# Talking-heads attention and a squared-ReLU FFN on one core: reciprocals by pairs, new lengths for SyncE in the planner, evictions on either engine, AV in one piece

## The chip, the cores and the metric

The kernel runs on one core of one Trainium2 chip. The metric is the device time in microseconds; a kernel's time is the median over several executions. One further execution is recorded by the hardware profiler, and every duration below is from that recording.

## The reference

Inputs are `q`, `k`, `v` (8 batches, 12 heads, 448 rows, 64 wide), two 12x12 head-mixing matrices and the two weight matrices of the FFN (768x2048, 2048x768).

```
scores = 0.125 * q @ k^T                       # per batch and head, 448 x 448
scores = einsum('bhij,hg->bgij', scores, w_pre)
attn   = exp(scores - max(scores)); attn /= sum(attn) + 1e-9
attn   = einsum('bhij,hg->bgij', attn, w_post)
x      = (attn @ v), heads side by side        # 3584 x 768
out    = (max(x @ w_in, 0) ** 2) @ w_out
```

## The kernel before

The 448 rows of a batch are cut into 45 **chunks** of ten rows (one of them has eight), and a chunk holds its rows for all twelve heads, 120 partitions by 448 keys. 8 batches make 360 chunks, numbered n. Each goes through a fixed chain (`chunk`, L734):

- TensorE mixes the heads (`f_m`, L774, into a bank of PSUM). Its input is an `sch` tile that SyncE's DMA has gathered from `snat`, the scores by heads (`relayout`, L686; the DMA is issued in `move`, L679). The scores come from `score` (L640) and are copied out of PSUM to `snat` on VectorE or ScalarE (L666). `snat` has two buffers, `sch` eleven. The 26 steps "direct" in batch 0 skip the relayout (L780).
- VectorE takes the row minimum of the negated scores (`f_max`, L785), ScalarE the exponential with its row sum (`f_exp`, L788; an instruction that reads the accumulator follows each), VectorE the reciprocal (`f_rc`, L794), GpSimd scales the second mixing matrix with it (`f_wq`, L797).
- TensorE multiplies by that, "AT", four matmuls (`f_at`, L804), and VectorE or ScalarE copies the result to `atb` (`f_ac`).

The tiles between the steps (`es`, `mn`, `sm`, `rc`, `wq`) have NE = 6 buffers each, so the mix of chunk n needs the AT of chunk n-6.

When the chunks of half a batch are through, `av` (L832) multiplies by `v` in three pieces of 16 matmuls (batch 0: smaller ones, more often). A piece fills one bank, and ScalarE copies it to `xt` (L853). The FFN runs over units of 128 or 256 columns of `xt` (`unit`, L879): first matmul (L896), ReLU on ScalarE (L909), square on GpSimd (L912), second matmul (L928), a copy to `osb` on VectorE (L943), store by SyncE. FFN matmuls have the lowest priority: they fill TensorE where no chunk is ready.

The order on each engine is written by a **planner** (`Planner.run`, L135), at build time. It replays all operations with a cost in ns, a latency, a priority and dependencies. At each point an engine takes the ready operation of least priority value. An operation with two costs, such as `{"DVE": 540, "ACT": 440}`, goes to whichever of the two engines takes it first. The chip then runs each engine's list in that order, whatever the real durations are: an instruction that waits holds up all that stand behind it on its engine. The planner's guess for the chunk's relayout on SyncE is 770 or 500 ns (L712). AHEAD (L43) says how many chunks ahead relayouts and scores are ranked.

TensorE's score matmuls of 64 rows work in row mode and AV's of 64 columns in column mode. The planner charges TURN = 95 ns for a change, and STAY lets TensorE, once in row mode, take further scores ahead of other work (L211 to L222). Where TensorE has nothing ready early in the run, the planner may put in idle matmuls (`still`, L1145). In banks, `MOST` caps the kinds, and an operation that needs several banks waits until all are free at once.

Of the kernel before, what the change touches and what calls it, by code (L numbers as in the profile page):

```python
# [24 lines left out]
CI = 10  # L25
# [9 lines left out]
NB = 4  # L35
# [6 lines left out]
NSCH = 11  # L42
AHEAD = 7.2  # L43
FIFO = 50
# [3 lines left out]
TURN = 95  # L48
STAY = 2
HOLD = "g"  # L50
# [65 lines left out]
class Planner:  # L116
# [18 lines left out]
    def run(self):  # L135
# [39 lines left out]
        while True:  # L175
            for eng, heap in ready.items():
# [24 lines left out]
                while heap:  # L201
                    item = heapq.heappop(heap)
                    op = item[2]
                    if op.eng is not None:
                        continue
                    wide = len(op.bank) > 1
                    if not fits(op) or (short and op.bank and op.bank[0][0] in HOLD):
                        short = short or wide
                        kept.append(item)
                        continue  # L210
                    if eng == "PE" and mode == ROWS and op.mode != ROWS and first is None:  # L211
                        first = item
                        kept.append(item)
                        continue
                    if first is not None:
                        if op.mode != ROWS or op.pri > first[0] + STAY:
                            kept.append(item)
                            if op.pri > first[0] + STAY:
                                op, item = first[2], first
                                kept.remove(first)  # L220
                            else:
                                continue  # L222
                    args = []
                    break
                else:
                    item = None
                    if first is not None:
                        kept.remove(first)
                        item, op, args = first, first[2], []
# [68 lines left out]
def kernel(  # L298
# [33 lines left out]
    mn = many(NE, "mn", [KC, 1], F32)  # L332
    sm = many(NE, "sm", [KC, 1], F32)
    rc = many(NE, "rc", [KC, 1], F32)
    wq = many(NE, "wq", [KC, H, CI], BF16)
# [227 lines left out]
    def x_tail(b):  # L563
        old = [score_ops[b - 1, 0, p] for p in range(NPAIR)]

        def turn():
            nc.sync.dma_start(
                out=zt[:, :, :], in_=qt[:, :, :].rearrange("p a c -> p (a c)"), transpose=True,
            )

        pri = b * NCHUNK - 15
        op = add("SP", 1250, pri, turn, [tail_in[b]] + old)
        done = add("TURN", 800, pri, lambda: None, [op], lat=6000)
        got_tail[b] = [done]
        for p in range(NPAIR):
            ready_tail[b, p] = done
# [8 lines left out]
    def x_piece(b, g):  # L585
# [30 lines left out]
        ]  # L616
        sk = add("SP", TURN_SP, pri, turn_k, ck + old)
        sq = add("SP", TURN_SP, pri, turn_q, cq + old)
        k_ = tk_op[2 * b + g] = add("TURN", 1500, pri, lambda: None, [sk], lat=6000)
# [66 lines left out]
    def relayout(b, c):  # L686
# [8 lines left out]
        if r == 2 and cc == 0:  # L695
            src_of[n] = schl
            here.append(move(n, pri, 700, deps + side.get(b - 1, []), schl[24:96, :], sn[120:126, :, :], lat))
            return
# [12 lines left out]
        for of, r0, r1, srcs in parts:  # L711
            ns = 770 if r1 - r0 > 90 else 500  # L712
            relay_of.setdefault(of, []).append(move(n, pri, ns, deps + old, src_of[n][r0:r1, :], srcs, lat))
# [20 lines left out]
    def chunk(b, c):  # L734
# [52 lines left out]
        def f_exp():  # L787
            nc.scalar.activation(  # L788
                out=es[i][0:rows, 0:S], in_=slots[mk][0:rows, 0:S], func=ACT.Exp, scale=-1.0,
                bias=mn[i][0:rows, 0:1], accum_out=sm[i][0:rows, 0:1],  # L790
            )

        def f_rc():
            nc.vector.reciprocal(out=rc[i][0:rows, :], in_=sm[i][0:rows, :])  # L794

        def f_wq():
            nc.gpsimd.tensor_scalar(  # L797
                out=wq[i][0:rows, :, 0:ns], in0=back[0:rows, :, 0:ns], scalar1=rc[i][0:rows, 0:1], scalar2=1.0,
                op0=ALU.mult, op1=ALU.mult,
            )  # L800
# [24 lines left out]
        e = exp_op[n] = add("ACT", 626, n + 0.4, f_exp, [x, at_op.get(n - NE), rc_op.get(n - NE)], lat=190, frees=mk)  # L825
        s_ = rc_op[n] = add("DVE", 75, n + 0.2, f_rc, [e, wq_op.get(n - NE)], lat=180)
        w = wq_op[n] = add("POOL", 370, n + 0.5, f_wq, [s_, at_op.get(n - NE)] + (backed if not far else []), lat=70)
# [3 lines left out]

    def av(b, half, g, x0, x1):  # L832
        to = [(max(c0, x0), t0 + max(x0 - c0, 0), min(c0 + w, x1) - max(c0, x0)) for c0, t0, w in spans(b % 2, half)]
        to = [span for span in to if span[2] > 0]
        key = ("g", "v", b, half, g, x0)

        def mms(slot):
            v_ = slot[:, :].rearrange("p (a c) -> p a c", a=2)
            for i in range(2):
                c2 = 2 * g + i  # L840
                for jb in range(NB):
                    for hh in range(2):
                        nc.tensor.matmul(  # L843
                            v_[64 * hh:64 * hh + 64, i, 0:x1 - x0],
                            lhsT=vs[:, 2 * c2 + hh, jb, :],
                            rhs=atb[half][:, jb, 2 * c2 + hh, x0:x1],
                            start=(jb == 0), stop=(jb == NB - 1),
                        )

        def evac():  # L850
            v_ = slots[key][:, :].rearrange("p (a c) -> p a c", a=2)
            for c0, t0, w in to:
                nc.scalar.copy(out=xt[:, 2 * g:2 * g + 2, t0:t0 + w], in_=v_[:, :, c0 - x0:c0 - x0 + w])  # L853

# [5 lines left out]
        if b >= 2:  # L860
# [4 lines left out]
        mm = add(  # L865
            "PE", 60 + 48 * (x1 - x0) // 14, pri, keep(key, mms), [ac_op[n] for n in cs] + v_in[b] + old, lat=200,
            bank=key, mode=COLS,
        )
        av_op.setdefault((b, half), []).append(mm)
        xc = add("ACT", 440 if len(to) == 1 else 650, pri, evac, [mm], lat=100, frees=key)  # L870
        for _, t0, w in to:
            xc_op.setdefault(b // 2, []).append((t0, t0 + w, xc))

# [5 lines left out]
    def unit(pair, ui):  # L879
# [11 lines left out]
        for f0 in range(0, FT, nf):  # L891
# [15 lines left out]

            def relu(key=key, gi=gi):
                nc.scalar.activation(out=hr[gi % 2][:, :], in_=slots[key][:, :], func=ACT.Relu)  # L909

# [6 lines left out]

            rl = add("ACT", 500, 0, relu, [end, hr_log[gi - 2] if gi >= 2 else None], lat=100, frees=key)
            sq = add("POOL", 1020, FILL, square, [rl] + old_o, lat=70)
            hr_log.append(sq)  # L920
            sq_op[ix].append(sq)
        for mt in range(w // 128):
            for nt in range(2):
# [17 lines left out]

                def evac(key=key, si=si, nt=nt):
                    nc.vector.tensor_copy(out=osb[si % 2][:, nt * 384:(nt + 1) * 384], in_=slots[key][:, 0:384])  # L943

                ev = add("DVE", 480, 0, evac, [end, st_op.get(si - 2)] + ([m_op[n_] for n_ in direct] if si < 2 else []), lat=100, frees=key)
                whole = not (z == W2B and mt == 1 and pair == B // 2 - 1)
                evs = evs + [ev] if nt == 1 and whole else [ev]
                if nt == 1 or not whole:
                    done = []
                    for rows, dst, o in pieces(pair, a + mt * 128, None if whole else nt):  # L950
                        def store(dst=dst, o=o, rows=rows, si=si, e0=0 if whole else nt * 384, e1=384 if not whole and nt == 0 else DMODEL):
                            nc.sync.dma_start(out=dst, in_=osb[si % 2][o:o + rows, e0:e1])
                        done.append(add("SP", 450 if rows <= CI else 850, FILL, store, evs))
                    st_op[si] = pl.moved("DMA", 8, 140, 130, 0, done, 1500)
# [105 lines left out]
    def first_batch():  # L1060
# [7 lines left out]
        for n, c in enumerate(ORDER0):  # L1068
# [16 lines left out]
            if c == C0[1]:  # L1085
                for g in range(3):
                    av(0, 0, g, 0, P_ROWS)
                unit(0, 0)
            if c == C0[2]:
                for g in range(3):  # L1090
                    av(0, 0, g, P_ROWS, XA)
            if c == C0[3]:
                for g in range(3):
                    av(0, 1, g, 0, P_ROWS)
                unit(0, 1)
        for g in range(3):
            av(0, 1, g, P_ROWS, XB)
        unit(0, 2)

    def next_batch(b):  # L1100
# [11 lines left out]
        for r in range(NJ + 1):  # L1112
            for p in groups(b, r):
                score(b, r, p)
            for c in range(C0[r], (C0 + [NCHUNK])[r + 1]):
                relayout(b, c)
                chunk(b, c)
                if c == C0[2]:
                    for g in range(3):
                        av(b, 0, g, 0, XA)  # L1120
                    unit(b // 2, 0 if b % 2 == 0 else last - 1)
                if b + 1 < B and c in (3, 6):
                    load_ahead(b + 1, n0 + c, 0 if c == 3 else 6)
        for g in range(3):
            av(b, 1, g, 0, XB)
        unit(b // 2, 1 if b % 2 == 0 else last)
# [59 lines left out]
```

## Time and profile before

| what | value |
|---|---|
| median of 3 runs | 587.76 us (587.71 to 588.72) |
| the profiled execution's own time | 588.38 us |
| its span, first to last instruction | 586.6 us |
| TensorE busy | 571.7 us (97%), 5809 matmuls |
| VectorE, ScalarE, GpSimd busy | 488.5, 469.6, 323.5 us |
| granted TensorE clock | 1.000 |

In a group of instructions the columns are line, engine, operation, output<-input, shape and count, then busy us and the mean ns of one. In the timeline the first two numbers are start and length in us, and what stands in brackets is the idle time before and what ended it. "PEld" is TensorE's weight load, "SPq" an instruction of SyncE that issues a DMA.

### The profile page before, as it was taken

How to read it: one execution, taken by the hardware profiler on the slowest of the kernel's cores; microseconds unless marked ns; L12 is line 12 of the kernel's file. 1: busy time of each engine (PE TensorE's matmuls, PEld its weight loads, DVE VectorE, ACT ScalarE, POOL GpSimd, SP SyncE). 2: the span in 40 equal slices, each digit the busy share in tenths (PEclk: the TensorE clock that was granted, in tenths of full speed). 3: DMA queues.
4: the chain of work that ended last, by engine and by line, in shares of the span. 5: the costliest groups of instructions: out<-in, count | busy, mean ns of one | idle time of the engine just before them, and what ended most of it. 6: DMA issues, size and time to landing. Idle time of an engine off the chain costs nothing.

```text
span 586.6 us, 17120 instructions
## 1 busy us (share of the span) xinstructions
PE 571.7 (97%) x5809; PEld 410.3 (70%) x5809; DVE 488.5 (83%) x1256; ACT 469.6 (80%) x1238; POOL 323.5 (55%) x592
## 2 busy tenths in 40 slices
PE   8999999999999999999999999999999999999996
PEld 5658666776677667667768676767757776767783
DVE  4899989987799897999898998999899897989201
ACT  2689998988888888787899889878888988888330
POOL 7366356655576347736586356834577444735340
PEclk9999999999999999999999999999999999999999
DMA  9989949964599549974398548964399545322021
GB/s 119 213 149 225 174 99 201 182 146 112 117 193 138 147 142 156 167 164 121 97 189 176 151 122 130 194 146 121 85 185 185 140 131 121 114 77 85 2 55 54
DMA packets 132996, 81.01 MB, mean 138 GB/s; under 512 B 60484, under 2 KB 127916, under 8 KB 132908
## 3 DMA queue, kind: packets, MB, share of 16 engines
q1 hardware_dynamic: 85340, 57.11, 40.1%
q0 software_dynamic: 47568, 22.81, 30.5%
q8 instruction: 45, 0.74, 0.5%
q14 instruction: 43, 0.35, 0.2%
HBM read 45.70 MB, written 11.01 MB: 97 GB/s over the span
## 4 chain that ended last, share of the span: by engine, by line
PE 78%; DMA 8%; DVE 6%; ACT 4%; issue 2%; POOL 2%; SPq 0%; DVEq 0%; ACTq 0%; POOLq 0%
PE bank L928 24%; PE bank L896 20%; PE bank L804 11%; PE bank L774 10%; PE bank L843 6%; PE bank L652 5%; DMA ks<-in_k_dram 4%; DMA sch<-snat 3%; ACT es L788 2%; DVE mn L785 2%; PE bank L780 1%; DVE snat L452 1%; DVE atb L452 1%; ACT hr L909 1%; PE bank L508 1%
## 5 line engine op out<-in xcount | busy, mean ns | idle before, releaser
L788 ACT ACTIVATE es<-bank,mn 120x448 bf16<-120x448 f32 (+1 forms) x360 | 229.9, 645 | 30.9 <-DVE mn L785 23.4
L797 POOL TENSOR_SCALAR wq<-wback,rc 120x120 bf16<-120x120 f32 (+1 forms) x347 | 125.8, 366 | 174.2 <-DVE rc L794 102.0
L785 DVE TENSOR_REDUCE mn<-bank 120x1 f32<-120x448 f32 (+1 forms) x360 | 210.6, 611 | 5.1 <-PE bank L774 2.4
L928 PE MATMUL bank<-w,h 128*128 128x384 bf16 x896 | 173.5, 325 | 0.3
L896 PE MATMUL bank<-xt,w 128*128 128x256 bf16 (+1 forms) x1632 | 165.0, 254 | 0.2
L452 DVE CAST atb<-bank 112x480 bf16<-112x480 f32 (+3 forms) x226 | 137.5, 619 | 27.6 <-PE bank L804 25.9
L896 PEld LDWEIGHTS <-w 128*128 128x128 bf16 x1632 | 135.6, 98 | 22.1 <-issue 3.6
L912 POOL TENSOR_TENSOR h<-hr 128x512 bf16<-128x512 f32 x112 | 116.2, 1039 | 48.9 <-ACT hr L909 46.2
L804 PEld LDWEIGHTS <-es 120*112 120x112 bf16 (+1 forms) x1440 | 114.8, 129 | 40.2 <-issue 10.2
L804 PE MATMUL bank<-wq,es 120*112 120x120 bf16 (+1 forms) x1440 | 127.5, 217 | 5.4 <-POOL wq L797 3.8
L928 PEld LDWEIGHTS <-h 128*128 128x128 bf16 x896 | 84.2, 97 | 54.6 <-issue 4.2
L774 PE MATMUL bank<-sch,wmix 120*128 120x448 bf16 x339 | 107.7, 353 | 0.8 <-DVE snat L452 0.6
L452 DVE CAST snat<-bank 128x448 bf16<-128x448 f32 x159 | 93.2, 613 | 6.1 <-DMA sch<-snat 3.1
L454 ACT CAST atb<-bank 112x480 bf16<-112x480 f32 (+3 forms) x158 | 84.0, 543 | 14.4 <-PE bank L804 13.5
L909 ACT ACTIVATE hr<-bank 128x512 f32<-128x512 f32 x112 | 67.3, 601 | 32.2 <-PE bank L896 25.9
L454 ACT CAST snat<-bank 128x448 bf16<-128x448 f32 x165 | 82.0, 550 | 8.6 <-PE bank L652 5.1
L788 ACT ACTIVATION_READ_ACCUMULATOR es<-bank,mn 120x1 f32 (+1 forms) x360 | 76.2, 212 | 0.0
L794 DVE RECIPROCAL rc<-sm 120x1 f32<-120x1 f32 (+1 forms) x360 | 53.5, 154 | 13.6 <-ACT es L788 10.8
L943 DVE COPY osb<-bank 128x384 f32<-128x384 f32 x56 | 30.9, 552 | 31.9 <-PE bank L928 31.5
L774 PEld LDWEIGHTS <-wmix 120*128 120x128 bf16 (+1 forms) x347 | 31.4, 97 | 20.1 <-issue 12.5
L843 PE MATMUL bank<-atb,vs 112*64 112x192 bf16 (+3 forms) x864 | 40.6, 250 | 0.1
L843 PEld LDWEIGHTS <-vs 112*64 112x64 bf16 x864 | 36.6, 110 | 4.0 <-issue 3.5
(60 smaller groups left out, 280.7 us busy)
## 6 DMA issues: line engine op xcount, KB each, us to landing
sch<-snat SPq DMA_DIRECT2D x324, 105.0 KB
out_dram<-osb SPq DMA_DIRECT2D x22, 360.0 KB
vs<-in_v_dram POOLq DMA_DIRECT2D x16, 336.0 KB, 7.7
ks<-in_k_dram POOLq DMA_DIRECT2D x14, 336.0 KB, 9.8
qs<-in_q_dram POOLq DMA_DIRECT2D x14, 288.0 KB, 9.1
w<-in_moe_w_in_dram POOLq DMA_DIRECT2D x6, 512.0 KB, 14.2
w<-in_moe_w_out_dram POOLq DMA_DIRECT2D x4, 768.0 KB, 21.6
out_dram<-osb SPq DMA_DIRECT2D x10, 192.0 KB
```

The costliest lines, as they stand in the source:

```text
L452: nc.vector.tensor_copy(out=out_, in_=in_)
L454: nc.scalar.copy(out=out_, in_=in_)
L774: nc.tensor.matmul(slot[:, 0:S], lhsT=wm[0:rows, :], rhs=src[0:rows, :], start=True, stop=True,)
L785: nc.vector.tensor_reduce(out=mn[i][0:rows, :], in_=slots[mk][0:rows, 0:S], axis=AX.X, op=ALU.min)
L788: nc.scalar.activation(out=es[i][0:rows, 0:S], in_=slots[mk][0:rows, 0:S], func=ACT.Exp, scale=-1.0, bias=mn[i][0:rows, 0:1], accum_out=sm ...
L797: nc.gpsimd.tensor_scalar(out=wq[i][0:rows, :, 0:ns], in0=back[0:rows, :, 0:ns], scalar1=rc[i][0:rows, 0:1], scalar2=1.0, op0=ALU.mult, op ...
L804: nc.tensor.matmul(slot[0:P_KEYS, jb * H * ns:(jb + 1) * H * ns], lhsT=es[i][0:rows, jb * P_KEYS:(jb + 1) * P_KEYS], rhs=wq[i][0:rows, :, ...
L843: nc.tensor.matmul(v_[64 * hh:64 * hh + 64, i, 0:x1 - x0], lhsT=vs[:, 2 * c2 + hh, jb, :], rhs=atb[half][:, jb, 2 * c2 + hh, x0:x1], start ...
L896: nc.tensor.matmul(slot[:, j * w:(j + 1) * w], lhsT=w1[c2][:, (f0 + j) * 128:(f0 + j + 1) * 128], rhs=xt[:, c2, a:z], start=(c2 == 0), sto ...
L909: nc.scalar.activation(out=hr[gi % 2][:, :], in_=slots[key][:, :], func=ACT.Relu)
L912: nc.gpsimd.tensor_tensor(out=h2_[:, f0:f0 + nf, 0:w], in0=hr[gi % 2][:, :].rearrange("p (f c) -> p f c", f=nf), in1=hr[gi % 2][:, :].rear ...
L928: nc.tensor.matmul(slot[:, 0:384], lhsT=h2_[:, ft, mt * 128:(mt + 1) * 128], rhs=w2[:, ft, nt * 384:(nt + 1) * 384], start=(ft == 0), stop ...
```

## The change

Five edits. (1) Chunks n and n+1 (n even) share `sm` and `rc` tiles with two columns; one reciprocal of 120x2 runs after both exponentials. (2) Planner costs of SyncE's instructions: relayout 770 to 860 and 500 to 590, the extra one 700 to 780, transposes 1250 to 1400 and 1500 to 1600..2300, stores 450 to 510 and 850 to 930; AHEAD 7.2 to 7.6. (3) ReLU, `xt` copies and `osb` copies may run on either engine. (4) From batch 3 (the fourth) on, AV is one operation that takes three banks. (5) STAY holds for column mode too, with 6.

```diff
-AHEAD = 7.2
+AHEAD = 7.6
-STAY = 2
+GS, ONE = [(0, 1, 2)], [(0,), (1,), (2,)]
+STAY = {ROWS: 2, COLS: 6}
...
-                    if eng == "PE" and mode == ROWS and op.mode != ROWS and first is None:
+                    if eng == "PE" and mode and op.mode != mode and first is None:
...
-                        if op.mode != ROWS or op.pri > first[0] + STAY:
+                        if op.mode != mode or op.pri > first[0] + STAY[mode]:
...
-        op = add("SP", 1250, pri, turn, [tail_in[b]] + old)
+        op = add("SP", 1400, pri, turn, [tail_in[b]] + old)
...
-        sk = add("SP", TURN_SP, pri, turn_k, ck + old)
-        sq = add("SP", TURN_SP, pri, turn_q, cq + old)
+        sk = add("SP", 2300 if b == 2 else TURN_SP + 300, pri, turn_k, ck + old)
+        sq = add("SP", 2000 if b == 2 else TURN_SP + 100, pri, turn_q, cq + old)
...
-            ns = 770 if r1 - r0 > 90 else 500
+            ns = 860 if r1 - r0 > 90 else 590
...
-            nc.vector.reciprocal(out=rc[i][0:rows, :], in_=sm[i][0:rows, :])
+            nc.vector.reciprocal(out=rc[i // 2][:, :], in_=sm[i // 2][:, :])
...
-        s_ = rc_op[n] = add("DVE", 75, n + 0.2, f_rc, [e, wq_op.get(n - NE)], lat=180)
+        if n % 2 == 0:
+            s_ = rc_op[n] = add("DVE", 77, n + 0.2, f_rc, [e, wq_op.get(n - NE), wq_op.get(n - NE + 1)], lat=180)
+        else:
+            s_ = rc_op[n] = rc_op[n - 1]
+            s_.left += 1
+            e.next.append(s_)
...
-        xc = add("ACT", 440 if len(to) == 1 else 650, pri, evac, [mm], lat=100, frees=key)
+        for g, key in zip(gs, keys):
+            xc = add(
+                {"ACT": 440, "DVE": 540} if len(to) == 1 else {"ACT": 650, "DVE": 750}, 0, pri,
+                lambda eng, g=g, key=key: evac(eng, g, key), [mm], lat=100, frees=key,
+            )
...
+            def relu(eng, key=key, gi=gi):
+                if eng == "DVE":
+                    nc.vector.tensor_scalar(
+                        out=hr[gi % 2][:, :], in0=slots[key][:, :], scalar1=0.0, scalar2=0.0, op0=ALU.max, op1=ALU.add,
+                    )
+                else:
+                    nc.scalar.activation(out=hr[gi % 2][:, :], in_=slots[key][:, :], func=ACT.Relu)
...
-            rl = add("ACT", 500, 0, relu, [end, hr_log[gi - 2] if gi >= 2 else None], lat=100, frees=key)
+            rl = add({"ACT": 500, "DVE": 590}, 0, 0, relu, [end, hr_log[gi - 2] if gi >= 2 else None], lat=100, frees=key)
...
-                ev = add("DVE", 480, 0, evac, [end, st_op.get(si - 2)] + ([m_op[n_] for n_ in direct] if si < 2 else []), lat=100, frees=key)
+                ev = add({"DVE": 480, "ACT": 440}, 0, 0, evac, [end, st_op.get(si - 2)] + ([m_op[n_] for n_ in direct] if si < 2 else []), lat=100, frees=key)
...
-                        done.append(add("SP", 450 if rows <= CI else 850, FILL, store, evs))
+                        done.append(add("SP", 510 if rows <= CI else 930, FILL, store, evs))
...
-                    for g in range(3):
-                        av(b, 0, g, 0, XA)
+                    for gs in GS if b >= 3 else ONE:
+                        av(b, 0, gs, 0, XA)
```

More of the change, by code (lines that the diff above doesn't have):

```diff
@@ L215, in run @@
                     if first is not None:
-                        if op.mode != ROWS or op.pri > first[0] + STAY:
+                        if op.mode != mode or op.pri > first[0] + STAY[mode]:
                             kept.append(item)
-                            if op.pri > first[0] + STAY:
+                            if op.pri > first[0] + STAY[mode]:
                                 op, item = first[2], first
@@ L332 @@
     mn = many(NE, "mn", [KC, 1], F32)
-    sm = many(NE, "sm", [KC, 1], F32)
-    rc = many(NE, "rc", [KC, 1], F32)
+    sm = many(NE // 2, "sm", [KC, 2], F32)
+    rc = many(NE // 2, "rc", [KC, 2], F32)
     wq = many(NE, "wq", [KC, H, CI], BF16)
@@ L696, in relayout @@
             src_of[n] = schl
-            here.append(move(n, pri, 700, deps + side.get(b - 1, []), schl[24:96, :], sn[120:126, :, :], lat))
+            here.append(move(n, pri, 780, deps + side.get(b - 1, []), schl[24:96, :], sn[120:126, :, :], lat))
             return
@@ L789, in f_exp @@
                 out=es[i][0:rows, 0:S], in_=slots[mk][0:rows, 0:S], func=ACT.Exp, scale=-1.0,
-                bias=mn[i][0:rows, 0:1], accum_out=sm[i][0:rows, 0:1],
+                bias=mn[i][0:rows, 0:1], accum_out=sm[i // 2][0:rows, i % 2:i % 2 + 1],
             )
         def f_rc():
-            nc.vector.reciprocal(out=rc[i][0:rows, :], in_=sm[i][0:rows, :])
+            nc.vector.reciprocal(out=rc[i // 2][:, :], in_=sm[i // 2][:, :])
         def f_wq():
             nc.gpsimd.tensor_scalar(
-                out=wq[i][0:rows, :, 0:ns], in0=back[0:rows, :, 0:ns], scalar1=rc[i][0:rows, 0:1], scalar2=1.0,
+                out=wq[i][0:rows, :, 0:ns], in0=back[0:rows, :, 0:ns], scalar1=rc[i // 2][0:rows, i % 2:i % 2 + 1], scalar2=1.0,
                 op0=ALU.mult, op1=ALU.mult,
@@ L830, in chunk, with av, mms, evac @@
         ac_op[n] = add({"DVE": 565 * len(where), "ACT": 600 * len(where)} if len(where) == 1 else {"DVE": 700, "ACT": 850}, 0, n + 1.6, f_ac, [a], lat=110, frees=ak)
-    def av(b, half, g, x0, x1):
+    def av(b, half, gs, x0, x1):
         to = [(max(c0, x0), t0 + max(x0 - c0, 0), min(c0 + w, x1) - max(c0, x0)) for c0, t0, w in spans(b % 2, half)]
         to = [span for span in to if span[2] > 0]
[L835 to L850, printed above, removed]
+        keys = [("g", "v", b, half, g, x0) for g in gs]
+        def mms(*got):
+            for g, slot in zip(gs, got):
+                v_ = slot[:, :].rearrange("p (a c) -> p a c", a=2)
+                for i in range(2):
+                    c2 = 2 * g + i
+                    for jb in range(NB):
+                        for hh in range(2):
+                            nc.tensor.matmul(
+                                v_[64 * hh:64 * hh + 64, i, 0:x1 - x0],
+                                lhsT=vs[:, 2 * c2 + hh, jb, :],
+                                rhs=atb[half][:, jb, 2 * c2 + hh, x0:x1],
+                                start=(jb == 0), stop=(jb == NB - 1),
+                            )
+        def evac(eng, g, key):
             v_ = slots[key][:, :].rearrange("p (a c) -> p a c", a=2)
             for c0, t0, w in to:
-                nc.scalar.copy(out=xt[:, 2 * g:2 * g + 2, t0:t0 + w], in_=v_[:, :, c0 - x0:c0 - x0 + w])
+                copy(eng, xt[:, 2 * g:2 * g + 2, t0:t0 + w], v_[:, :, c0 - x0:c0 - x0 + w])
         def touches(c):
@@ L865, in av @@
         mm = add(
-            "PE", 60 + 48 * (x1 - x0) // 14, pri, keep(key, mms), [ac_op[n] for n in cs] + v_in[b] + old, lat=200,
-            bank=key, mode=COLS,
+            "PE", 60 + 48 * (x1 - x0) // 14 * len(gs), pri, keep(keys, mms), [ac_op[n] for n in cs] + v_in[b] + old, lat=200,
+            bank=keys, mode=COLS,
         )
         av_op.setdefault((b, half), []).append(mm)
-        xc = add("ACT", 440 if len(to) == 1 else 650, pri, evac, [mm], lat=100, frees=key)
-        for _, t0, w in to:
-            xc_op.setdefault(b // 2, []).append((t0, t0 + w, xc))
+        for g, key in zip(gs, keys):
[3 more added lines that the diff above has]
+            )
+            for _, t0, w in to:
+                xc_op.setdefault(b // 2, []).append((t0, t0 + w, xc))
     def units_of(pair):
@@ L906, in unit @@
             gi = len(hr_log)
-            def relu(key=key, gi=gi):
-                nc.scalar.activation(out=hr[gi % 2][:, :], in_=slots[key][:, :], func=ACT.Relu)
+            def relu(eng, key=key, gi=gi):
+                if eng == "DVE":
+                    nc.vector.tensor_scalar(
+                        out=hr[gi % 2][:, :], in0=slots[key][:, :], scalar1=0.0, scalar2=0.0, op0=ALU.max, op1=ALU.add,
+                    )
+                else:
+                    nc.scalar.activation(out=hr[gi % 2][:, :], in_=slots[key][:, :], func=ACT.Relu)
             def square(gi=gi, f0=f0):
@@ L940, in unit, with evac @@
                 si = ix_store[0]
-                def evac(key=key, si=si, nt=nt):
-                    nc.vector.tensor_copy(out=osb[si % 2][:, nt * 384:(nt + 1) * 384], in_=slots[key][:, 0:384])
-                ev = add("DVE", 480, 0, evac, [end, st_op.get(si - 2)] + ([m_op[n_] for n_ in direct] if si < 2 else []), lat=100, frees=key)
+                def evac(eng, key=key, si=si, nt=nt):
+                    copy(eng, osb[si % 2][:, nt * 384:(nt + 1) * 384], slots[key][:, 0:384])
+                ev = add({"DVE": 480, "ACT": 440}, 0, 0, evac, [end, st_op.get(si - 2)] + ([m_op[n_] for n_ in direct] if si < 2 else []), lat=100, frees=key)
                 whole = not (z == W2B and mt == 1 and pair == B // 2 - 1)
@@ L1085, in first_batch @@
             if c == C0[1]:
-                for g in range(3):
-                    av(0, 0, g, 0, P_ROWS)
+                for gs in ONE:
+                    av(0, 0, gs, 0, P_ROWS)
                 unit(0, 0)
             if c == C0[2]:
-                for g in range(3):
-                    av(0, 0, g, P_ROWS, XA)
+                for gs in ONE:
+                    av(0, 0, gs, P_ROWS, XA)
             if c == C0[3]:
-                for g in range(3):
-                    av(0, 1, g, 0, P_ROWS)
+                for gs in ONE:
+                    av(0, 1, gs, 0, P_ROWS)
                 unit(0, 1)
-        for g in range(3):
-            av(0, 1, g, P_ROWS, XB)
+        for gs in ONE:
+            av(0, 1, gs, P_ROWS, XB)
         unit(0, 2)
@@ L1118, in next_batch @@
                 if c == C0[2]:
-                    for g in range(3):
-                        av(b, 0, g, 0, XA)
+                    for gs in GS if b >= 3 else ONE:
+                        av(b, 0, gs, 0, XA)
                     unit(b // 2, 0 if b % 2 == 0 else last - 1)
@@ L1123, in next_batch @@
                     load_ahead(b + 1, n0 + c, 0 if c == 3 else 6)
-        for g in range(3):
-            av(b, 1, g, 0, XB)
+        for gs in GS if b >= 3 else ONE:
+            av(b, 1, gs, 0, XB)
         unit(b // 2, 1 if b % 2 == 0 else last)
```

## The prediction

> **What bounds the kernel now.** I read the busy shares first, then busy time by stage, then the timeline of the worst stage. The page:
>
> ```profile
> PE 571.7 (97%) x5809; PEld 410.3 (70%) x5809; DVE 488.5 (83%) x1256; ACT 469.6 (80%) x1238; POOL 323.5 (55%) x592
> ```
>
> TensorE is the bound, so only its own work and its waits count. Its work: in the chain of waits 12 matmuls of the first FFN product at 256 columns take 1.31 us (109 ns each), 64 of the second take 10.41 (163 ns). With the spacings that the timeline shows for the others (52 ns a matmul of AT, 189 a mix, 95 a row-mode score, some 40 us for AV) all 5809 come to about 529 us. The 182 changes of tile mode cost 0.145 us each (starts of matmuls across a change, less the spacing), 26 us. 1.1 us lie before the first matmul and 5.0 behind the start of the last. That is 561 of 586.6; of the other 25, 10 fall into the first 20 us (loads, and matmuls spaced 0.37 instead of 0.19 us). The rest are waits and small gaps. Busy time in stretches (length; then PE, PEld, DVE, ACT, POOL):
>
> ```profile
> 20.00:47.00 27.00, 25.41 (x232) 16.82 (x231) 26.06 (x77) 22.44 (x61) 12.80 (x26) 1.00 1.03 182
> 47.00:82.00 35.00, 33.35 (x530) 25.26 (x530) 32.24 (x85) 33.57 (x94) 19.08 (x36) 1.00 0.97 182
> 82.00:130.00 48.00, 47.93 (x522) 33.41 (x520) 42.81 (x112) 43.20 (x116) 27.64 (x54) 1.00 0.89 162
> 130.00:145.00 15.00, 13.84 (x125) 9.63 (x122) 11.82 (x31) 11.97 (x32) 9.01 (x14) 1.00 0.46 127
> 145.00:215.00 70.00, 69.50 (x706) 49.24 (x706) 61.71 (x159) 61.14 (x163) 38.57 (x73) 1.00 0.79 144
> 215.00:245.00 30.00, 28.16 (x278) 20.60 (x277) 25.54 (x67) 24.59 (x64) 22.00 (x38) 1.00 0.97 159
> 245.00:350.00 105.00, 105.00 (x1054) 76.06 (x1054) 97.81 (x248) 89.91 (x242) 57.15 (x108) 1.00 0.71 146
> ```
>
> TensorE is idle for 1.6, 1.7, 0.1, 1.2, 0.5, 1.8 and 0.0 us, and after 350 us for 0.5. A matmul's record hides up to 0.2 us of each wait; by starts, gaps of over 0.14 us beyond spacing and mode change sum to 2.3, 3.3, 0.4, 1.7, 1.3, 2.9, 0.1 and 1.6: **13.7 us**. That is all that any reordering can win in the middle, and past 245 us almost nothing is left. In 20 to 47 us VectorE is busy 97%: the chain of waits runs through it there. The stretch from 130 us is of another kind:
>
> ```profile
> 135.68 4.29 SPq L680 DMA_DIRECT2D sch<-snat  x5
> ...
> 138.21 0.97 ACT L454 CAST snat<-bank 128x448 bf16<-128x448 f32 x2 [1.90 <-DMA sch<-snat]
> 138.23 1.16 DVE L452 CAST snat<-bank 128x448 bf16<-128x448 f32 x2 [2.21 <-DMA sch<-snat]
> 138.80 0.49 PEld L804 LDWEIGHTS <-es 120*112 120x112 bf16 x8 [1.13 <-ACT snat L454]
> ```
>
> SyncE issues five relayouts in 4.29 us, 858 ns each; the planner counted 770. So `snat` is freed later than planned, both copying engines stand 2 us at an instruction that wants its buffer, and TensorE behind them 1.1.
>
> **The change, part by part.** The sum goes against the profiled execution's 588.38 us; the median shown is 0.62 lower.
>
> *TensorE's own list.* The built order holds the same matmuls plus four idle ones (35 to 39; they fill waits, 0). Mode changes fall from 182 to 178: 4 x 0.145 = **-0.6 us** (bounds 0 and -0.8). That is all of the column STAY and of AV in one piece, since in 17 of 19 visits to column mode the 48 matmuls of three pieces already stood together; what was to be gathered is gathered. The Trainium skill, "TensorEngine Tiling (Array Packing)", Key Properties, says that a change of tiling mode drains TensorE; the 0.145 us agree, and by that rule too the saving is four drains. Holding three banks at once is cost 0: FFN work covers it, and without that cover it is at most the 0.4 us of one eviction for each of ten gathered AVs, whose users stand behind other FFN work in the order.
>
> *SyncE's lengths.* Nothing is removed; the planner now spaces relayouts as the chip does (858 against 860). What should go are gaps that follow a late relayout: those at 130 to 145 us (1.7), at 145 to 215 (1.3; the chain there leads through relayouts of 7.56 and 1.56 us), and 1.4 of the 3.3 in 47 to 82, behind one of 7.32. Together 4.4 us. But the transfers stay, and SyncE's queue was issuing 18 of 20 us at 200 to 220 us, so the next burst is late by whatever else lands late. I take half: **-2.2 us** (bounds -4.4 and +1, one such gap newly made).
>
> *Reciprocals by pairs.* A reciprocal's record is 154 ns, but VectorE starts the next instruction 70 ns on (135.33 and 135.40 in the timeline). 180 fewer free 12.6 us of VectorE, 0.9 of it in the stretch where it is the chain (13 pairs x 70 ns). Against that, every even chunk waits for the odd one's sum: the two reciprocals were 1.34 us apart in the mean, and half of the ATs stood under 0.9 us behind their `wq`. In the new order the AT moves back too: between mix and AT of an even chunk stand 6.8 us of TensorE's work in the median (5.4 before), of an odd one 6.0 (5.5). The ring of six covers it: chunks are 1.51 us apart, six are 9.05. Only in batch 0, where few fillers exist, may it cost; the five shortest stretches there, against a chain of 2.4 us (0.61 + 0.65 + 0.2 + 0.15 + 0.37 and hand-overs), lack 0.9 us more than before. The 0.9 freed and the 0.9 lacked cancel: **0** (bounds -0.9 and +1.5).
>
> *ReLU, `xt`, `osb` on either engine.* The order puts 86 of 112 ReLUs on VectorE, 29 of 63 `xt` copies too, 22 of 56 `osb` copies on ScalarE; 29 fewer `atb` and 7 fewer `snat` copies on VectorE. Starts back to back: a copy of 384 takes VectorE 463 ns, of 448 522, so a ReLU of 512 is estimated at 581 (ScalarE: 478). VectorE: 86 x 0.581 + 12.5 for `xt` - 12.6 for reciprocals - 29 x 0.56 - 7 x 0.522 - 22 x 0.463 = **+20 us**; ScalarE -27. In the trace VectorE thus goes from 467 to 487 us of slots, no bound over the span. But to the 45th row minimum it is 68.1 before and 71.4 after, to the 90th 123.4 and 128.5. FFN work covers that from batch 1 on, not where VectorE is 92% to 97% busy. There are no ReLUs before 47 us; from 47 to 82 us ScalarE, which gives them up, is the fuller of the two (33.57 of 35 against 32.24). I go by that row: **0** (bounds -1.5, if the freer ScalarE shortens waits, and +3.3, all of batch 0's rise). The Trainium skill, "VectorE: DVE Perf Modes", Why PSUM operands drop a tier, holds fp32 from PSUM at one element a cycle; it speaks against moving ReLU there, and the slower VectorE row (463 for 384) agrees. It changes nothing in the 581.
>
> Sum: -0.6 - 2.2 + 0 + 0 = **-2.8 us**: 585.6 for a profiled execution, **585.0** against the median.
>
> **Rivals.**
>
> *VectorE becomes the chain in batches 0 and 1 (slower).* To the 90th row minimum it has 138 us (11 to 149 us); its slots go from 89% to 93% of that. ReLUs in its queue wait for the end of FFN matmuls (ScalarE spent 9.6 us so between 20 and 550 us, at 0.5 each), and row minima stand behind them. Price: half of the 5.1 us of added slots, 2.5, and the even chunks' 0.9; the gain at SyncE is lost to it, -0.6 stays: +2.8, or 590.5; with half of SyncE's gain 589.4. It decides if over half of the added slots land where TensorE has no FFN work. For: 97% and 92% busy; against: the planner sees these lengths, and ScalarE takes other copies.
>
> *Nothing moves (the relabelled lengths shift gaps but do not close them).* Those at 215 to 245 us (2.9) follow a load of `k` that lands 9.8 us after issue, which no edit touches; if SyncE's gaps reappear elsewhere, -0.6 remains: 587.2.
>
> *All goes well.* SyncE's whole 4.4, 0.9 at the reciprocals, 1.5 from ScalarE, 0.6: -7.4, 580.4. For: later stages show gaps near 0 with the same work; against: half of the gaps are in batch 0, where VectorE gets more.
>
> **How the numbers follow.** Forecast (583 to 586.5) 0.50; all well (under 583) 0.14; nothing (586.5 to 588.9) 0.17; VectorE (over 588.9) 0.19. The range to hold 8 in 10: 581.8 to 589.2, which leaves out the ends of "all well" and of VectorE's case. A difference of under 0.2% (1.2 us) could not be told from no change here: faster (under 586.6) 0.64, same 0.17, slower 0.19.
>
> **What would show it.** Right: TensorE's 26 us of mode changes nearly unchanged; in a stretch at 130 to 145 us no copy to `snat` idle for 2 us behind a relayout; VectorE's busy time up by some 10 us in spite of 120 fewer instructions, ScalarE's down by 30; the ReLU's mean on VectorE near 670 ns; a `k` load still stalling around 225 to 240 us. Wrong: row minima queued behind waiting ReLUs, and batch 1's first row minimum, now at 82.0 us, at 84 or later (VectorE's case); ATs that wait for `wq` more than the page's few us (pairs); new idle of `snat` copies behind DMA (SyncE).

## The result, and the profile after

The changed kernel takes 585.15 us in the median of 17 runs (584.19 to 587.03), the kernel before 587.76 (586.21 to 590.83); the ratio is 0.9950, 95% interval 0.9937 to 0.9963. The forecast was 585.0 us, and faster. The profiled execution took 585.32 us, its span is 583.5 (586.6 before).

The busy shares of the changed kernel:

```profile
PE 569.2 (98%) x5813; PEld 407.5 (70%) x5813; DVE 510.9 (88%) x1136; ACT 443.2 (76%) x1179; POOL 321.7 (55%) x591
```

VectorE's busy time rose by 22.4 us with 120 instructions fewer, ScalarE's fell by 26.4. Busy time by stretches, in the columns used before:

```profile
20.00:47.00 27.00, 25.38 (x234) 16.27 (x233) 25.79 (x70) 22.65 (x62) 12.82 (x25) 1.00 1.05 188
47.00:82.00 35.00, 32.80 (x527) 25.04 (x525) 33.34 (x78) 30.60 (x84) 18.49 (x35) 1.00 0.95 176
82.00:130.00 48.00, 46.87 (x521) 32.94 (x519) 45.53 (x104) 41.24 (x112) 28.19 (x57) 1.00 0.95 167
130.00:145.00 15.00, 15.00 (x142) 10.95 (x140) 14.60 (x32) 12.31 (x32) 9.92 (x15) 1.00 0.40 109
145.00:215.00 70.00, 69.63 (x705) 48.95 (x704) 65.45 (x146) 57.07 (x154) 38.20 (x73) 1.00 0.71 151
215.00:245.00 30.00, 29.21 (x291) 21.45 (x290) 28.84 (x63) 24.84 (x66) 23.02 (x39) 1.00 0.96 161
```

TensorE's idle time went from 1.2 us to nothing at 130 to 145 us and from 1.8 to 0.8 at 215 to 245; it rose from 1.7 to 2.2 at 47 to 82 and from 0.1 to 1.1 at 82 to 130. At 138 us, where copies to `snat` had stood for 2 us, the timeline now reads:

```profile
136.66 5.17 SPq L681 DMA_DIRECT2D sch<-snat  x6
...
138.07 1.14 DVE L453 CAST snat<-bank 128x448 bf16<-128x448 f32 x2
...
138.29 0.96 ACT L455 CAST snat<-bank 128x448 bf16<-128x448 f32 x2
```

No bracket stands behind either copy: neither waits for a relayout. Six relayouts took 5.17 us, 862 ns each, just what the planner now counts.

Most of the rise at 82 to 130 us is at one place. The timeline there:

```profile
81.58 0.69 DVE L921 TENSOR_SCALAR hr<-bank 128x512 f32<-128x512 f32 x1 [0.74 <-PE bank L907]
...
82.19 0.65 DVE L453 CAST atb<-bank 112x480 bf16<-112x480 f32 x1
...
82.67 0.23 ACT L789 ACTIVATION_READ_ACCUMULATOR es<-bank,mn 120x1 f32 x1
82.75 1.14 DVE L786 TENSOR_REDUCE mn<-bank 120x1 f32<-120x448 f32 x2
...
83.82 0.15 DVE L795 RECIPROCAL rc<-sm 120x2 f32<-120x2 f32 x1
...
84.17 0.70 POOL L798 TENSOR_SCALAR wq<-wback,rc 120x120 bf16<-120x120 f32 x2 [0.78 <-DVE rc L795]
...
84.58 0.37 PE L805 MATMUL bank<-wq,es 120*112 120x120 bf16 x4 [1.09 <-POOL wq L798]
```

VectorE stands 0.74 us at a ReLU, with row minima behind it; the reciprocal then serves two chunks at once, and TensorE waits 1.09 us for the first `wq`. That is the forecast's slower rival, at one place and 1.1 us large. It is not the even chunk waiting for its partner: ScalarE had read out the partner's row sum by 82.90 us (82.67 and 0.23), and VectorE came to the reciprocal at 83.82, behind the row minima. Over the whole span TensorE's matmuls waited less for `wq` than before. The row of "AT" in the two pages, before and after, with the idle time of TensorE and what ended it at the end:

```profile
L804 PE MATMUL bank<-wq,es 120*112 120x120 bf16 (+1 forms) x1440 | 127.5, 217 | 5.4 <-POOL wq L797 3.8
```

```profile
L805 PE MATMUL bank<-wq,es 120*112 120x120 bf16 (+1 forms) x1440 | 118.3, 217 | 3.2 <-POOL wq L798 2.6
```

By the prediction's measure (gaps of over 0.14 us between starts of matmuls, beyond spacing and mode change), in us by stretch, for the two kernels and the runs told below. TensorE's matmuls themselves sum to 526.8 to 527.6 us in all of them, the mode changes to 25.9 to 27.7.

| kernel | median us | 20-82 | 82-115 | 115-150 | 150-350 | from 350 | sum |
|---|---|---|---|---|---|---|---|
| before | 587.76 | 5.6 | 0.4 | 1.7 | 4.4 | 1.6 | 13.7 |
| changed | 585.15 | 6.2 | 1.5 | 0.0 | 2.4 | 1.7 | 11.8 |
| before + SyncE's lengths | 591.22 | 6.0 | 0.0 | 0.2 | 8.0 | 2.5 | 16.7 |
| before, nudge 628 | 588.14 | 5.0 | 0.0 | 0.2 | 6.9 | 0.7 | 12.8 |
| changed, nudge 628 | 588.19 | 6.3 | 2.2 | 0.0 | 1.5 | 6.2 | 16.2 |
| changed, nudge 624 | 587.57 | 4.8 | 1.1 | 2.5 | 1.1 | 2.9 | 12.4 |
| changed, old lengths | 594.37 | 6.0 | 1.5 | 6.0 | 3.3 | 2.5 | 19.4 |
| old lengths, nudge 628 | 585.87 | 5.9 | 2.5 | 2.4 | 0.3 | 0.2 | 11.2 |
| old lengths, nudge 624 | 592.12 | 6.9 | 0.2 | 3.8 | 2.9 | 2.5 | 16.2 |
| old lengths, stores left out | 586.85 | 6.0 | 1.8 | 0.5 | 2.7 | 1.7 | 12.8 |
| changed order, two reciprocals | 585.48 | 6.6 | 1.6 | 0.0 | 2.3 | 1.8 | 12.2 |
| changed order, ReLU on ScalarE | 588.59 | 7.0 | 2.4 | 0.2 | 4.4 | 2.4 | 16.4 |
| new lengths early only, nudge 628 | 588.39 | 6.3 | 1.3 | 0.0 | 3.3 | 2.4 | 13.4 |
| changed, engines fixed | 589.90 | 6.5 | 0.2 | 0.3 | 4.7 | 2.9 | 14.6 |

One profiled execution stands behind each row, and the executions of a kernel spread by 1 to 7 us, so a row need not add up to its median, and gaps of a few tenths are not to be read. From the kernel before to the changed one these gaps fall by 1.9 us, while the span falls by 3.1: smaller gaps and spacings, which this measure leaves out, make up the rest.

### The profile page after: what moved, and what is told of

It reads as the page before. It is cut to its first block, busy times and chain, and to the rows that moved or that the text cites. A ratio compares the mean times of both kernels' runs of the same rounds, so it can differ in the third digit from the quotient of the medians.

```text
span 583.5 us, 16716 instructions
## 1 busy us (share of the span) xinstructions
PE 569.2 (98%) x5813; PEld 407.5 (70%) x5813; DVE 510.9 (88%) x1136; ACT 443.2 (76%) x1179; POOL 321.7 (55%) x591
## 4 chain that ended last, share of the span: by engine, by line
PE 88%; DVE 6%; DMA 3%; issue 1%; ACT 1%; POOL 1%; DVEq 0%; POOLq 0%; ACTq 0%
PE bank L944 25%; PE bank L907 24%; PE bank L805 13%; PE bank L775 11%; PE bank L850 6%; PE bank L653 6%; PE bank L781 2%; DVE mn L786 2%; DMA sch<-snat 2%; DMA ks<-in_k_dram 1%; DVE atb L453 1%; DVE snat L453 1%; PE bank L509 1%; ACT es L789 0%; DVE hr L921 0%
## 5 line engine op out<-in xcount | busy, mean ns | idle before, releaser
L789 ACT ACTIVATE es<-bank,mn 120x448 bf16<-120x448 f32 x360 | 228.7, 641 | 48.4 <-DVE mn L786 44.3
L786 DVE TENSOR_REDUCE mn<-bank 120x1 f32<-120x448 f32 x360 | 209.8, 611 | 4.9 <-PE bank L781 2.9
L805 PEld LDWEIGHTS <-es 120*112 120x112 bf16 (+1 forms) x1440 | 107.5, 130 | 30.9 <-ACT es L789 7.0
L453 DVE CAST atb<-bank 112x480 bf16<-112x480 f32 (+2 forms) x197 | 118.5, 610 | 12.1 <-PE bank L805 10.7
L805 PE MATMUL bank<-wq,es 120*112 120x120 bf16 (+1 forms) x1440 | 118.3, 217 | 3.2 <-POOL wq L798 2.6
L455 ACT CAST atb<-bank 112x480 bf16<-112x480 f32 (+3 forms) x187 | 99.7, 541 | 14.5 <-PE bank L805 13.8
L789 ACT ACTIVATION_READ_ACCUMULATOR es<-bank,mn 120x1 f32 x360 | 74.3, 206 | 0.0
L921 DVE TENSOR_SCALAR hr<-bank 128x512 f32<-128x512 f32 x86 | 59.1, 687 | 16.4 <-PE bank L907 14.7
L653 PE MATMUL bank<-kt,qz 64*128 64x448 bf16 x276 | 39.5, 354 | 0.8 <-ACT es L789 0.6
L453 DVE COPY osb<-bank 128x384 f32<-128x384 f32 x34 | 18.8, 552 | 17.6 <-PE bank L944 17.2
```

The costliest lines, as they stand in the source:

```text
L453: nc.vector.tensor_copy(out=out_, in_=in_)
L455: nc.scalar.copy(out=out_, in_=in_)
L653: nc.tensor.matmul(slot[:, 0:S], lhsT=lhsT, rhs=kt[i][half, :, at_, :], start=True, stop=True)
L786: nc.vector.tensor_reduce(out=mn[i][0:rows, :], in_=slots[mk][0:rows, 0:S], axis=AX.X, op=ALU.min)
L789: nc.scalar.activation(out=es[i][0:rows, 0:S], in_=slots[mk][0:rows, 0:S], func=ACT.Exp, scale=-1.0, bias=mn[i][0:rows, 0:1], accum_out=sm ...
L805: nc.tensor.matmul(slot[0:P_KEYS, jb * H * ns:(jb + 1) * H * ns], lhsT=es[i][0:rows, jb * P_KEYS:(jb + 1) * P_KEYS], rhs=wq[i][0:rows, :, ...
```

## The experiments

The theory at the start: the gain is made at SyncE, since its planner lengths are now those of the chip. Rival A: it is made on VectorE and ScalarE. Rival B: every new order of the planner lands somewhere within some us, and this one landed well. Such an order is called a draw below. Each ratio is against the kernel before, measured again beside the run (medians 587.84 to 588.12 us); the changed kernel's 585.15 us was not measured again beside them.

**SyncE's lengths alone, on the kernel before.**

```diff
-            ns = 770 if r1 - r0 > 90 else 500
+            ns = 860 if r1 - r0 > 90 else 590
```

(and the other SyncE costs of the change; AHEAD stays)

> The kernel before with SyncE's new planner lengths alone (relayouts, transposes, stores; AHEAD stays 7.2). Theory (the gaps behind late relayouts carry the gain): about 2.2 us faster than before, 585 to 586.5, and no copy to snat idle for 2 us at 130 to 145 us. Rival A (the gain comes from the work that may go to either engine and the paired reciprocals): within 0.7 us of before. Rival B (every new order of the planner lands somewhere within some us, whatever the edit): anything from 585 to 590, unrelated to relayouts.

Measured: 591.22 us, ratio to before 1.0061 (1.0038 to 1.0084). Slower, where the theory wanted 2 us faster, and beyond rival B's 585 to 590 too. The gap at 138 us did go (1.7 to 0.2 at 115 to 150), but 3.6 us came up at 150 to 350. In that kernel's timeline a late relayout now stands elsewhere:

```profile
169.73 0.62 DVE L452 CAST snat<-bank 128x448 bf16<-128x448 f32 x1 [1.35 <-DMA sch<-snat]
...
170.41 0.42 PE L804 MATMUL bank<-wq,es 120*112 120x120 bf16 x4 [0.67 <-DVE snat L452]
```

**The change without SyncE's lengths** (the diff above in reverse, on the changed kernel).

> The changed kernel with SyncE's old planner lengths; all else stays. Theory: the gain falls from 2.6 us to about 0.5, so 587 to 587.8, with copies to snat idle behind relayouts again. Rival A: stays near 585. Rival B: anything from 583 to 588.

Measured: 594.37 us, ratio 1.0117 (1.0098 to 1.0135); 9.2 us behind the changed kernel, more than the theory's 2, and outside both rivals' figures. SyncE's queue in this kernel:

```profile
136.37 0.83 SPq L968 DMA_DIRECT2D out_dram<-osb  x1
...
137.30 0.78 SPq L681 DMA_DIRECT2D sch<-snat  x1
...
138.13 0.48 SPq L968 DMA_DIRECT2D out_dram<-osb  x1
...
138.73 2.54 SPq L681 DMA_DIRECT2D sch<-snat  x3
...
140.76 0.97 ACT L455 CAST snat<-bank 128x448 bf16<-128x448 f32 x2 [3.07 <-DMA out_dram<-osb]
140.78 1.15 DVE L453 CAST snat<-bank 128x448 bf16<-128x448 f32 x2 [3.68 <-DMA out_dram<-osb]
...
141.34 0.35 PE L775 MATMUL bank<-sch,wmix 120*128 120x448 bf16 x1 [1.98 <-ACT snat L455]
```

Two stores lie before and between the relayouts of a burst, both copying engines stand over 3 us, TensorE 2. The profile names the store as releaser, but in the program a copy to `snat` waits for the relayouts that read this buffer, not for stores; that a relayout behind the store held it is likely, and was not read out.

**A nudge without meaning**, on both kernels: the planner's cost of the exponential is 628 in place of 626.

```diff
-        e = exp_op[n] = add("ACT", 626, n + 0.4, f_exp, ...
+        e = exp_op[n] = add("ACT", 628, n + 0.4, f_exp, ...
```

> The kernel before with the planner's cost of the exponential at 628 in place of 626 ns: an edit without meaning, which gives the planner another order. Theory and rival A: within 0.7 us of before (587 to 588.5). Rival B: over 1 us away from before, in either direction.

Measured: 588.14 us, ratio 1.0001 (0.9986 to 1.0015). The time stays, as the theory and rival A had it, but not the gaps: 115 to 150 us has 0.2 in place of 1.7, with the old lengths, and 150 to 350 has 6.9 in place of 4.4. Not all of this execution's time is the order's. In one stretch the granted clock (the 0.50 in the first line) was half, and twelve matmuls of the first FFN product took 2.52 us there, where the timelines of other runs show 1.47:

```profile
244.40:247.80 3.40, 3.40 (x19) 2.29 (x17) 2.15 (x7) 2.87 (x9) 1.61 (x3) 0.50 1.48 117
```

```profile
244.13 2.52 PE L896 MATMUL bank<-xt,w 128*128 128x256 bf16 x12
```

Half the clock for 3.4 us is an estimated loss of 1.7 us.

> The changed kernel with the same meaningless nudge, 628 in place of 626 ns. Theory and rival A: within 0.7 us of the changed kernel (584.5 to 586). Rival B: over 1 us away from it.

Measured: 588.19 us, ratio to before 1.0004 (0.9982 to 1.0027): the whole gain is gone by a change of 2 ns in a number that only the planner reads. This is what rival B said. The profiled execution took 590.47 us, 2.3 over the median. Its new gaps lie behind late transfers again; the timeline of this kernel at 472 us, with the new lengths:

```profile
470.41 1.38 SPq L968 DMA_DIRECT2D out_dram<-osb  x2
...
471.92 3.42 SPq L681 DMA_DIRECT2D sch<-snat  x4
...
472.84 0.62 DVE L453 CAST snat<-bank 128x448 bf16<-128x448 f32 x1 [2.00 <-DMA sch<-snat]
...
473.51 0.54 PE L775 MATMUL bank<-sch,wmix 120*128 120x448 bf16 x2 [1.75 <-DVE snat L453]
```

**Old lengths under two nudges, new ones under the second**, to tell the lengths from the draw (same two edits, combined).

> SyncE's old lengths again, under the nudge of 628 ns for the exponential. SyncE theory: old lengths are worse under any nudge, so over 588.2 (the changed kernel under the same nudge), by 2 us or more. Re-roll theory (every order lands somewhere within some us): between 584 and 595, as likely under 588.2 as over it. Under both, what the run loses should stand in the trace as copies or transposes that wait for a late DMA.

> The same with 624 ns. SyncE theory: again 588 or more. Re-roll theory: anywhere between 584 and 595.

> The changed kernel (new lengths) under the nudge of 624 ns, the partner of the run with old lengths and 624 ns (592.1). Re-roll theory: between 584 and 590, so the changed kernel itself is one draw of some. Local theory (the new lengths do close the gaps that follow late relayouts at 120 to 145 us, which stood in all three orders with old lengths and these edits, and other late transfers decide the rest): no gap over 0.14 us of TensorE between 130 and 145 us, and no copy to snat waiting for a DMA there; the time under 592.

Measured: 585.87 (ratio 0.9960, 0.9945 to 0.9976), 592.12 (1.0057, 1.0036 to 1.0077) and 587.57 us (1.0006, 0.9985 to 1.0026). The old lengths under 628 beat the new ones under the same nudge by 2.3 us, so "worse under any nudge" falls. Three orders with new lengths take 585.15, 587.57 and 588.19 (mean 587.0), three with old ones 585.87, 592.12 and 594.37 (mean 590.8): the difference of means is 3.8 us, with three draws each too few for a claim. Part of it goes with the clock: of the ten executions with old lengths under 624, the six with a mean granted clock of 0.989 to 0.991 took 592.0 to 594.5 us, the four with 0.993 or more 589.3 to 591.2. At one place the sides differ more: from 115 to 150 us the old lengths have gaps of 6.0, 2.4 and 3.8 us, the new ones 0.0, 0.0 and 2.5. (The kernel before has 1.7 and, nudged, 0.2 with old lengths, and 0.2 with new ones.) The 2.5 is a miss of the local theory, though its conditions were met: there a copy to `snat` waited 2.96 us behind seven relayouts at 118 to 124 us, just ahead of the stretch of 130 to 145 that I had named.

```profile
118.40 5.95 SPq L681 DMA_DIRECT2D sch<-snat  x7
...
122.29 0.97 ACT L455 CAST snat<-bank 128x448 bf16<-128x448 f32 x2 [2.96 <-DMA sch<-snat]
```

**SyncE's queue relieved, order kept.** In the kernel of 594.37 us all stores but those of the last pair of batches are left out; no engine's order changes.

```diff
-                            nc.sync.dma_start(out=dst, in_=osb[si % 2][o:o + rows, e0:e1])
+                            if pair == B // 2 - 1:
+                                nc.sync.dma_start(out=dst, in_=osb[si % 2][o:o + rows, e0:e1])
```

> The changed kernel with SyncE's old lengths (594.4 us), in the same order on every engine, with the stores of the first three pairs of batches left out, so three quarters of the output are not written: SyncE's queue loses 0.4 to 0.9 us for each of 42 issues. If SyncE's queue, late against the plan, makes the gaps: those of 120 to 145 us (7.5 us by starts) shrink to under 2, and the time falls by 4 to 7 us, to 587 to 590. If the gaps come from the order itself or from the loads: at most 1.5 us faster.

Measured: 586.85 us, 7.5 us less, where 4 to 7 were expected; the gaps of 115 to 150 us fall from 6.0 to 0.5. (The 7.5 us of gaps in the expectation count from 82 us on, 1.5 of them before 115.) Busy time of TensorE (the second number) in that stretch, first with the stores, then without:

```profile
115.00:150.00 35.00, 30.20 (x293) 21.41 (x291) 27.31 (x62) 24.11 (x66) 16.04 (x30) 1.00 0.60 132
```

```profile
115.00:150.00 35.00, 34.60 (x341) 24.85 (x339) 33.64 (x76) 29.70 (x81) 19.16 (x37) 1.00 0.51 119
```

4.4 of the 7.5 us come back in this one stretch, so the stores did make those gaps. By which way is not told apart, since the edit takes away three things: the stores' issue time on SyncE, ahead of the relayouts; their bytes; and the wait of a copy to `osb` until the store that reads this buffer has landed. That third wait stood in the same stretch of the kernel with the stores, 3.35 us on ScalarE, with TensorE behind it:

```profile
121.27 0.48 ACT L455 COPY osb<-bank 128x384 f32<-128x384 f32 x1 [3.35 <-DMA out_dram<-osb]
...
121.80 0.35 PE L775 MATMUL bank<-sch,wmix 120*128 120x448 bf16 x1 [0.99 <-ACT osb L455]
```

**VectorE loaded, order kept.** In the changed kernel two reciprocals stand where the paired one was.

```diff
-            nc.vector.reciprocal(out=rc[i // 2][:, :], in_=sm[i // 2][:, :])
+            nc.vector.reciprocal(out=rc[i // 2][:, 0:1], in_=sm[i // 2][:, 0:1])
+            nc.vector.reciprocal(out=rc[i // 2][:, 1:2], in_=sm[i // 2][:, 1:2])
```

> The changed kernel's order kept on every engine; only, in the place of each paired reciprocal two single ones are issued, 180 instructions more on VectorE, some 12.6 us of its slots. Theory (VectorE's slots are covered, the gaps of TensorE come from late transfers): within 0.7 us of 585.15. Rival (VectorE is the chain in batches 0 and 1, and lightening it carries the gain): 1.5 to 3 us slower than the changed kernel.

Measured: 585.48 us, ratio to before 0.9954 (0.9939 to 0.9969): as fast as the changed kernel (0.9950). Its row of the page beside the changed kernel's 510.9 us of VectorE:

```profile
PE 566.8 (97%) x5813; PEld 406.5 (70%) x5813; DVE 518.3 (89%) x1316; ACT 443.8 (76%) x1179; POOL 323.1 (55%) x591
```

180 instructions more cost nothing that can be measured. The slots saved by the pairs have cover; what the wait of an even chunk costs, the other half of that edit, is not told apart by this.

**ReLUs on ScalarE, order kept.** The 86 that the plan gives to VectorE are issued on ScalarE at the same places (`relu` always calls `nc.scalar.activation`).

> The changed kernel's order kept; the 86 ReLUs planned on VectorE are issued on ScalarE at the same places: VectorE loses 50 us of slots, ScalarE gains 41. If VectorE is the chain: faster than 585.15 by 1 us or more. Theory: VectorE has cover and ScalarE's queue now stands behind the plan, so slower, by 1 to 6 us, with exponentials queued behind ReLUs that wait for the FFN's matmuls.

Measured: 588.59 us, ratio to before 1.0013 (0.9997 to 1.0028), so 3.4 us behind the changed kernel, although VectorE has 46 us less to do (464.7 busy). VectorE was not the chain over the span; a ScalarE behind its plan costs. ScalarE's waits at ReLUs for the first FFN product are 7.1 us in all (3.8 before the swap); how much of the loss comes from exponentials queued behind these 3.3 us was not traced. TensorE's gaps rise in small pieces from 47 us on.

**Engines fixed as before, planned anew** (ReLU and `xt` copies on ScalarE, `osb` copies on VectorE; the rest of the change stays).

> The changed kernel planned anew with ReLU and xt copies on ScalarE alone and osb copies on VectorE alone, as before. If the freedom of engines carries the gain: 587.5 or more, with ScalarE back at some 470 us busy and exponentials queued behind ReLUs. If it carries nothing: 584 to 589, no further from the changed kernel than the nudges went (3 us).

Measured: 589.90 us, ratio 1.0032 (1.0012 to 1.0052). 1.7 to 4.8 us slower than each of the three orders in which the engines are free. One draw against three: it leans to a gain from the freedom, and does not settle it.

**An attempt at speed**: new lengths up to batch 2, old ones from batch 3 on, nudge 628, to join the good halves of two orders (`ns = 860 if b < 3 else 770`, and so on).

> A version for speed, under the nudge of 628: new SyncE lengths up to batch 2, where the order with old ones had its gaps (4.8 us at 82 to 145 us), old ones from batch 3 on, where that order had almost none. If orders keep their good parts: 582 to 584, the fastest so far. Re-roll theory: another draw, 584 to 592.

Measured: 588.39 us, ratio 1.0003 (0.9985 to 1.0021). The first part kept its 0.0 at 115 to 150 us; from 150 us on gaps of 5.7 us stand where the old lengths had 0.5. The good part of the other order was not kept: from the first difference on, another order followed. No version here beats the changed kernel.

## Why the prediction was right, point by point

The number was right to 0.2 us, by the place that it named for the main term, and by luck in what it took that term to be.

*What bounds the kernel.* Right, and the base of the rest: the work and the two ends are the same in all orders to within 1 us, and times differ mostly by gaps. Mostly, since the mode changes range over 1.8 us and the first 20 us over 1.6. The forecast said that 13.7 us of gaps are all that can be won, and nothing past 245 us; the changed kernel has 11.8.

*TensorE's list, -0.6.* The mode changes fell to 178 as read from the order, but cost 27.0 us in place of 26.3, so +0.7: other waits stand at them. The step counted them right and priced them as if nothing else could wait there. The 0.6 us that it added to the forecast were not gained.

*SyncE's lengths, -2.2.* Between the two traces the gaps fell by 2.5 us at 130 to 215 us and rose by 0.3 at 47 to 82: -2.2, and at 138 us by the mechanism named, a copy to `snat` no longer behind a late relayout. But the sentence that the lengths close such gaps fails as a rule: alone they made the kernel before 3.1 us slower, a 2 ns nudge took the whole gain, and one order with the old lengths is nearly as fast (585.87 us). That the two numbers agree is luck too: they cover the named stretches alone, and what the other stretches gave and took (-1.3 at 215 to 245 us, +1.1 at 82 to 130) was forecast as 0. What the runs show in its place: the stores cost TensorE up to 7.5 us in one order; with the new lengths gaps were smaller around 115 to 150 us in the draws made, too few to call it a rule; and where the next late transfer falls is a draw.

*Reciprocals by pairs, 0.* The cover named for VectorE's slots was shown by two reciprocals at the same places. The wait of the even chunk was not seen to cost anything: TensorE's matmuls of AT waited 2.6 us for `wq` in place of 3.8, and the 1.1 us at 84 us stand behind VectorE's queue. It was not priced by a run of its own.

*Either engine, 0.* VectorE's slots were forecast at +20 us and its busy time, among the signs, up by only some 10; it rose by 22.4. ScalarE's fell by 26.4 (30 forecast), and the ReLU's mean is 687 ns (670 forecast). That the move is free for the time was not shown; the run with engines fixed leans to a gain.

*Loads, 0.* The term left out, and a sign that failed: a load of `k` was to go on stalling at 225 to 240 us. Gaps at 215 to 245 us fell by 1.3 us, without an edit that touches them; the wait for a late load of `k` that stood there (1.7 us on VectorE) is gone in the new order, and in the changed kernel under the nudge of 628 such waits come to 8.4 us on GpSimd over the span.

*Rivals.* "VectorE becomes the chain": batch 1 began 1.3 us late (83.3 for 82.0), and 20 to 130 us has 1.7 us more of gaps; after that it was made good. Priced at 1.6 to 2.8 us over before, it was too dear. "Nothing moves": for the edits as such this is nearest to the truth, since the mean over three draws of the change is 587.0 us against 587.8 and 588.1 for the two of before, and that mean was not separated from no change.

What stays open: whether the lengths are worth 3.8 us in the mean, and whether the stores cost by their issue time, their bytes or the copies to `osb` that wait for them; the AV and STAY edits and AHEAD were not tried by themselves.

## What to carry to other kernels

Where a planner writes the order, one time of one order measures the draw as much as the edit: nudge a number that has no meaning, on both sides, before an effect of a few us is put down to its cause. To price an edit on the chip, keep the order and change only what is issued (two reciprocals for one, stores left out); that gave clearer answers here than planning anew, though an instruction left out can take several waits with it, as the stores did. When the bound engine's work is the same in all versions, look for the few instructions elsewhere that stand in brackets behind a DMA: much of what differed between the orders here stood there.

## What the hardware showed unexpectedly

With the same order, 42 store issues less on SyncE's queue, with the waits that hang on them, took 7.5 us off a kernel whose TensorE is busy 96% of the time, though its 16 DMA engines had room in the stretch where most of it came back (0.60 busy). One order also spreads by the granted clock: of the twelve executions of the kernel before under the nudge of 628, the three with a mean granted clock of 0.997 took 586.2 to 586.5 us, the five with 0.993 587.6 to 588.7, the four with 0.990 to 0.992 588.6 to 589.9. (The spread of 7 us of the changed kernel under that nudge does not follow its clock.) And the first 20 us of every kernel hold 8.9 to 10.5 us of gaps and slow spacing, whatever the order: no edit here touched them.
